# A folded projection product spread over three column groups, last output tiles finished one by one, and a new instruction order

## The chip, the cores and the metric

The kernel runs on one NeuronCore of a Trainium2 chip. Its engines are TensorE (PE in the profile; its weight loads are listed as PEld), VectorE (DVE), ScalarE (ACT), GpSimd (POOL), and SyncE (SP), which here only issues the DMAs. The metric is the device time of one execution in microseconds, lower is better. The median of three runs before the change is 456.12 us (455.83 to 457.48).

## The reference, cut to what matters

Three stages follow each other, on a batch of 2, 768 tokens, 512 channels, all in float32.

```python
# 1. block attention, 8 heads of 64: a window of +-15 keys and 24 block summaries
a = softmax(concat(mask(q @ k.T / 8), q @ k_blockmax.T / 8 + log(32)))
x = a @ concat(v, v_blockmean)
# 2. four causal attention experts, the best two of each token, gated
out = sum_over_chosen_e(w_e * (softmax(causal(x@wq[e] @ (x@wk[e]).T / 8)) @ (x@wv[e]) @ wo[e]))
# 3. mixer: a rank-32 product over the tokens, then an MLP of width 2048
h = (out.T @ U @ V).T          # U is 768 x 32, V is 32 x 768
u = out + h
y = u + relu(u @ w_ch1) @ w_ch2
```

The kernel folds `wo` into what follows it: the rank-32 product is taken on the experts' 256 concatenated head outputs (`C`, 256 x 768 per batch), and `wo @ w_ch1` is computed once. "Folded projection product" below is `U.T @ C.T`, a 32 x 256 result that sums over the 768 tokens.

## The kernel before, in words

Everything is unrolled into some 700 **parts**, small functions of one to twelve **steps** each (a Python generator; a step ends at each `yield`). `at(...)` numbers the parts in the order in which the program names them. The table `TIMES` holds, for each part, the position of each of its steps in one global order, and the instructions are issued in that order. So each engine's instruction stream, and the queue of DMAs on SP, is what the table says; an engine runs its stream strictly in order and waits on semaphores where data isn't ready. `BANKS` names for each part the PSUM bank (of eight, 128 x 512 floats each) that it writes. The constants in `Y` and `Z` give start values for the positions and have no effect where the tables are filled, as they are here.

The parts that matter below, with the line of their TensorE instructions in the profile:

- `vsum` (L333, then L340): block sums of the values of one head pair: 12 products of 128 columns, whose outputs go by turns to the four 32-partition groups of one bank; a copy and a small product add the four groups.
- `a_scores` (L385), `a_trans` (L396), `a_pv` (L408), `a_out` (L424): one 128-query slot of the first attention; 48 slots.
- `qk_proj` (L620), `v_proj` (L569): projections of the experts; after `qk_proj` ACT and DVE split the result in two, and POOL makes four copies (L236).
- `s_row` (L651), `s_norm` (POOL, L675), `t_bank` (L684), `pv` (L704): an expert's attention. `pv` writes by turns to two 64-partition groups of a bank.
- `c_nat` (L722), `a_mat` (L732), `c_add` (L742): the rank-32 product, once per batch. `a_mat` is the folded product: for each of six token tiles a stationary of 128 x 32 (`Usb`) and a moving 128 x 256, accumulated in partitions 0 to 31 of one bank. ACT copies the result twice (L734, L735), DVE takes the rest of it (L739, shown under the helper's line L239), and `c_add` uses all three.
- `w1c` (L497): products that fold `wo` into `w_ch1`; `w1_split`, `w2_split`, `wo_split`, `late_woT`, `v_stack`: splits of loaded weights over DVE, ACT and POOL.
- `resid` (L832), `one` (L810, with ACT L815 and DVE L817), `two` (L823): the MLP. `resid` starts the output bank of a token tile, `one(b, ff, j)` makes 128 hidden channels for 384 tokens, `two(b, ff, j)` adds them to the three token tiles of half `j`. `store` (ACT L843 for even tiles, DVE L845 for odd ones) copies an output bank to SBUF and issues its DMA (L847).

Loads of the first attention, per head pair, by their shapes: keys 416 KB, queries 2 x 192 KB, values 585 KB (for the first pair in two halves of 292.5 KB; the keys there in 144 + 272 KB). Constants: 128 + 180 + 39 KB.

Of the kernel before, what the change touches and what calls it, by code (L numbers as in the profile page):

```python
# [35 lines left out]
def f(ap):  # L36
# [9 lines left out]
         s4=0.55, wc=2.8, cc=1.4, cl=0.4, t3=6.0, t4=5.0, pm0=2.45, pm1=2.09, one=1.3, rl=0.75, rd=0.4, lf=30.0,  # L46
         ls=8.0, lw=-5.0, rs=1.3, rsp=0.4, sto=2.0)
TIMES = [
# [137 lines left out]
N_LAST = 2  # L186
# [4 lines left out]
def tile_block_attention_moe_mixer(ctx: ExitStack, tc: tile.TileContext, qT, kP, vW, vB, wm, woT, wo,  # L191
# [644 lines left out]
    def store(b, t):  # L836
# [5 lines left out]
        if t % 2 == 0:  # L842
            act.copy(sb, ob)  # L843
        else:
            dve.tensor_copy(sb, ob)  # L845
# [240 lines left out]
```

## Time and profile before

| | |
|---|---|
| median of 3 runs | 456.12 us (455.83 to 457.48) |
| the profiled execution's own time | 454.69 us |
| span of its instructions | 452.9 us |
| PE busy | 435.3 us, 96% of the span |
| DVE, ACT, POOL busy | 227.9, 218.3, 179.1 us |
| granted TensorE clock, mean | 0.998 |

The span runs from the first to the last instruction; 1.8 us of the execution's own time lie around it. Busy time is the time in which an engine has an instruction under way. The profile's chain of waits follows the work that ended last back to the start.

### The profile page before, as it was taken

The numbers are of one execution on the slowest core, as the hardware profiler recorded it, in microseconds if no ns is written. First come the engines' busy times: TensorE is split into PE (matmuls) and PEld (weight loads), VectorE is DVE, ScalarE is ACT, GpSimd is POOL, SyncE is SP. The second block draws the span as 40 slices with busy tenths as digits, with TensorE's granted clock in tenths as the row PEclk, the third lists the DMA queues.
The fourth block names the chain that finished last, engine by engine and source line by source line (L and its number), as shares of the span: only waits on it lengthen the run. The fifth ranks groups of instructions, "written<-read, shape, count | busy, mean of one in ns | idle before, by whom it ended". The sixth has DMA issues, their size and how long they took to land.

```text
span 452.9 us, 8633 instructions
## 1 busy us (share of the span) xinstructions
PE 435.3 (96%) x3224; PEld 377.5 (83%) x3224; DVE 227.9 (50%) x629; ACT 218.3 (48%) x578; POOL 179.1 (40%) x252
## 2 busy tenths in 40 slices
PE   1899999999999999899999999999999999999996
PEld 1687898999889887687989889899888888888884
DVE  4578755766557779767884544433322112112112
ACT  3578755756756778787564444434221111111111
POOL 7869853348645799762353143223110000000000
PEclk9999999999999999999999999999999999999999
DMA  8977730000000032253254343302110100000003
GB/s 219 245 214 200 219 88 4 2 1 19 1 2 1 1 111 92 74 187 116 92 168 144 111 150 128 111 31 54 40 69 25 46 2 0 0 1 0 1 0 139
DMA packets 14329, 35.19 MB, mean 78 GB/s; under 512 B 1872, under 2 KB 2896, under 8 KB 14288
## 3 DMA queue, kind: packets, MB, share of 16 engines
q1 hardware_dynamic: 14288, 34.65, 25.4%
q8 instruction: 25, 0.41, 0.4%
q14 instruction: 16, 0.13, 0.1%
HBM read 31.50 MB, written 3.15 MB: 77 GB/s over the span
## 4 chain that ended last, share of the span: by engine, by line
PE 92%; POOL 2%; DMA 2%; DVE 1%; SPq 1%; issue 0%; ACT 0%; DVEq 0%; POOLq 0%; ACTq 0%
PE ps L823 29%; PE ps L810 15%; PE ps L620 7%; PE ps L497 5%; PE ps L385 5%; PE ps L704 4%; PE ps L651 4%; PE ps L569 4%; PE ps L832 4%; PE ps L684 3%; PE ps L408 3%; PE ps L396 3%; PE ps L333 2%; DMA vb<-in_vW_dram 2%; PE ps L424 1%; PE ps L732 1%
## 5 line engine op out<-in xcount | busy, mean ns | idle before, releaser
L817 DVE SCALAR_TENSOR_TENSOR a<-ps,a 128x384 fp32r<-128x384 f32 x64 | 35.1, 555 | 118.4 <-ACT a L815 118.4
L815 ACT ACTIVATE a<-ps 128x384 fp32r<-128x384 f32 x64 | 31.2, 490 | 117.6 <-PE ps L810 62.6
L810 PE MATMUL ps<-x,w1h 128*128 128x384 f32 x256 | 73.5, 337 | 0.1
L823 PE MATMUL ps<-m,a 128*128 128x512 f32 x216 | 52.4, 392 | 0.0
L810 PEld LDWEIGHTS ps<-x,w1h 128*128 128x128 f32 x256 | 47.0, 188 | 2.2 <-DVE a L817 0.4
L823 PEld LDWEIGHTS ps<-m,a 128*128 128x128 f32 x216 | 40.3, 188 | 7.8
L810 PE MATMUL ps<-x,w1l 128*128 128x384 f32 x128 | 43.1, 336 | 0.0
L236 POOL TENSOR_SCALAR a<-a 64x384 fp32r<-64x384 f32 x64 | 33.6, 525 | 23.9 <-ACT a L625 19.5
L620 PE MATMUL ps<-x,m 128*128 128x384 f32 x192 | 36.9, 341 | 0.0
L620 PEld LDWEIGHTS ps<-x,m 128*128 128x128 f32 x192 | 33.1, 188 | 0.5 <-DVE gmx L608 0.2
L651 PE MATMUL ps<-a 128*128 128x384 f32 (+4 forms) x128 | 28.0, 338 | 1.4 <-POOL a L236 1.4
L675 POOL TENSOR_SCALAR ex<-ex,rs,gate 128x256 f32<-128x256 f32 (+5 forms) x36 | 25.9, 726 | 6.0 <-PE ps L704 3.2
L823 PE MATMUL ps<-vb,a 128*128 128x512 f32 x108 | 26.4, 392 | 0.0
L823 PE MATMUL ps<-v,a 128*128 128x512 f32 x108 | 26.4, 395 | 0.0
L257 DVE SCALAR_TENSOR_TENSOR x<-x 128x256 uint32<-128x256 uint32 (+3 forms) x38 | 23.0, 610 | 5.3 <-ACT x L255 5.1
L659 DVE CUSTOM_DVE_ANT_0 ex<-ps,cc 128x512 f32<-128x512 f32 (+5 forms) x36 | 21.1, 597 | 9.1 <-PE ps L651 4.6
L810 PEld LDWEIGHTS ps<-x,w1l 128*128 128x128 f32 x128 | 24.0, 188 | 1.7
L662 ACT ACTIVATE ex<-ex,nmx 128x512 f32<-128x512 f32 (+5 forms) x36 | 23.3, 647 | 3.4 <-DVE nmx L659 3.1
L823 PEld LDWEIGHTS ps<-v,a 128*128 128x128 f32 x108 | 20.2, 188 | 4.2
L388 DVE TENSOR_REDUCE nmx<-ps 128x2 f32<-128x240 f32 x48 | 18.8, 403 | 9.0 <-PE ps L385 7.7
L823 PEld LDWEIGHTS ps<-vb,a 128*128 128x128 f32 x108 | 20.1, 188 | 3.7
L651 PEld LDWEIGHTS ps<-a 128*128 128x128 f32 x128 | 19.9, 189 | 3.5 <-POOL a L236 1.7
(215 smaller groups left out, 924.1 us busy)
## 6 DMA issues: line engine op xcount, KB each, us to landing
x<-in_w_dram SPq DMA_DIRECT2D x16, 512.0 KB, 3.8
x<-in_w_dram SPq DMA_DIRECT2D x20, 256.0 KB, 2.7
vb<-in_vW_dram SPq DMA_DIRECT2D x5, 585.0 KB, 4.7
a<-in_kP_dram SPq DMA_DIRECT2D x7, 416.0 KB, 5.7
out_dram<-a SPq DMA_DIRECT2D x10, 256.0 KB, 2.2
x<-in_wm_dram SPq DMA_DIRECT2D x4, 386.0 KB, 7.0
a<-in_w_dram SPq DMA_DIRECT2D x6, 256.0 KB, 3.1
tb<-in_w_dram SPq DMA_DIRECT2D x6, 256.0 KB, 3.4
```

Source lines behind the costliest of these rows:

```text
L236: pool.tensor_scalar(dst, src, 1.0, 0.0, op0=ALU.mult, op1=ALU.add)
L257: dve.scalar_tensor_tensor(low, high, 3, low, op0=ALU.logical_shift_left, op1=ALU.bitwise_or)
L385: pe.matmul(scb[64 * u:64 * u + 64, hh], QAT[p % NK][hh][:, QT * (2 * t + u):QT * (2 * t + u) + QT], KWT[p % 2][hh][:, 2 * t + u, :], star ...
L497: pe.matmul(acc, wo[k][:, int(a == 2), 128 * c:128 * c + 128], w[k][:, int(a == 1)], start=j == 0, stop=j == 11)
L620: pe.matmul(acc, (WML if wl else WMH)[k][:, 128 * e:128 * e + 128], xt(b, k, xl)[:, c], start=n == 0, stop=n == 11)
L651: pe.matmul(flat[:, base + c0:base + c1], QS[u][:, 128 * i:128 * i + 128], kk[:, c0:c1], start=x == 0, stop=x == 1)
L662: act.activation(ex[:, 0:W], ex[:, 0:W], AF.Exp, bias=nmx, scale=-1.0, accum_out=sums)
L675: pool.tensor_scalar(ex, ex, rs[:, i % 2:i % 2 + 1], gate[b][:, i, e:e + 1], op0=ALU.mult, op1=ALU.mult)
L810: pe.matmul(acc, (W1L if wl else W1H)[ff // 2][:, c, 128 * (ff % 2):128 * (ff % 2) + 128], cp(b, c, xl)[:, o], start=n == 0, stop=n == 5)
L815: act.activation(h, acc, AF.Relu)
L817: dve.scalar_tensor_tensor(l, acc, 0.0, f(h), op0=ALU.max, op1=ALU.subtract)
L823: pe.matmul(out_bank(b, 3 * j + t), a[:, 128 * t:128 * t + 128], w, start=False, stop=ff == 15 and x == 2, skip_group_check=True)
```

## The change

Three edits. (1) `a_mat` sends token tile t to partition group 32 * (t % 3), so three accumulations of two products each take the place of one of six. The three partial results are then added: ACT copies the second to SBUF, DVE adds the first and that copy, then the third; ACT's two copies and DVE's remainder read the SBUF sum instead of PSUM. (2) For batch 1, half 1, the last two `two` parts are cut into one per token tile (`last_two`), and the store of tile 5 is cut into two halves of columns, one copied by ACT and one by DVE. (3) `TIMES` and `BANKS` are replaced as a whole; `t3` changes with them and has no effect of its own.

```diff
-         s4=0.55, wc=2.8, cc=1.4, cl=0.4, t3=6.0, t4=5.0, ...
+         s4=0.55, wc=2.8, cc=1.4, cl=0.4, t3=14.0, t4=5.0, ...
 TIMES = [
...
 BANKS = [
...
     def a_mat(b, bk):
         AST[b] = ast = region("ast", 256)
-        acc = bk[0:32, 0:256]
         for t in range(NT):
-            pe.matmul(acc, Usb[:, t, :], CNAT[b][:, t, :], start=t == 0, stop=t == NT - 1)
-        yield 2 * Y["chl"]
-        act.copy(ast[0:32, :], acc)
-        act.copy(ast[32:64, :], acc)
-        yield Y["chl"]
-        lo_dve(ast[64:96, :], acc, ast[0:32, :])
+            g = 32 * (t % 3)
+            pe.matmul(bk[g:g + 32, 0:256], Usb[:, t, :], CNAT[b][:, t, :], start=t < 3, stop=t >= 3, skip_group_check=True)
+        yield 0.001
+        part, total = (sm.tile([32, 256], F32, name=n, tag=n, bufs=1) for n in ("part", "total"))
+        act.copy(part, bk[32:64, 0:256])
+        yield 0.001
+        dve.tensor_tensor(total, bk[0:32, 0:256], part, op=ALU.add)
+        dve.tensor_tensor(total, bk[64:96, 0:256], total, op=ALU.add)
+        yield 0.001
+        act.copy(ast[0:32, :], total)
+        act.copy(ast[32:64, :], total)
+        yield 0.001
+        lo_dve(ast[64:96, :], total, ast[0:32, :])
...
-    def store(b, t):
+    def store(b, t, on=None, c=slice(0, DM)):
...
+    def last_two(ff, t):
+        mlp2(1, ff, 1, hl[1, ff, 1], (t,))
...
+                if b and j and ff >= 16 - N_LAST:
+                    for t in range(3):
+                        at(T + P * 31 + 0.3 * (N_LAST * t + ff - 16 + N_LAST), last_two, ff, t)
+                else:
+                    at(T + P * u, two, b, ff, j)
...
+            if b and i == NT - 1:
+                at(t, store, b, i, act, slice(0, DM // 2))
+                at(t + 0.01, store, b, i, dve, slice(DM // 2, DM))
+            else:
+                at(t, store, b, i)
```

Read from the two tables, in order of issue, at the places that the prediction speaks of (q0a is the first half of pair 0's queries, and so on):

```
SP at the start, before: cst k0a k0b cst2 q0a vB q0b v0a k1 v0b q1a v1 q1b
                 after:  cst k0a k0b cst2 k1 vB v0a v0b q0a q0b v1 q1a q1b
PE at the start, before: a_scores 0, 1, vsum 0 (L333), a_trans 0, vsum 0 (L340), a_scores 3, 2, 5, a_trans 1, a_scores 4, vsum 1
                 after:  vsum 0 (L333), vsum 0 (L340), a_scores 1, 0, 3, 2, 5, 4, vsum 1, a_trans 0, 1, 3
PE after a_mat 0, before: pv 7 0, pv 7 1, pv 7 2, c_add 0      after: w1c 1 1, pv 7 0, pv 7 2, pv 7 1, c_add 0
PE after a_mat 1, before: resid 0 0, one 0 0 0, c_add 1        after: one 0 0 1, resid 0 0, two 0 0 0, c_add 1
PE at the end, before: two(14, half 1) and two(15, half 1), each tiles 3, 4, 5
               after:  two(14) tile 3, then 14/5, 15/5, 14/4, 15/4, 15/3
copies of the last tiles, before: ACT 4; DVE 5, then 3         after: DVE and ACT 5 in halves, ACT 4, DVE 3
TensorE parts from qk_proj(5, 0) to s_row(7, 5), before: 45    after: 49
```

## Rows read from the trace of the kernel before

**Rows 1.** The page, part 4: shares of the chain that ended last, by engine.

```profile
PE 92%; POOL 2%; DMA 2%; DVE 1%; SPq 1%; issue 0%; ACT 0%; DVEq 0%; POOLq 0%; ACTq 0%
```

**Rows 2.** Windows by stage: stretch, its length, busy us (instructions) per engine, clock, DMA.

```profile
0.00:9.20 9.20, 0.00 (x0) 0.00 (x0) 4.34 (x7) 3.32 (x11) 6.84 (x14) 1.00 0.76 209
9.20:18.70 9.50, 7.84 (x82) 5.76 (x84) 4.47 (x11) 4.00 (x13) 8.56 (x15) 1.00 1.03 251
...
171.00:184.00 13.00, 11.05 (x77) 8.35 (x77) 10.55 (x30) 10.90 (x30) 11.73 (x19) 1.00 0.29 102
...
202.00:215.00 13.00, 13.00 (x81) 8.86 (x81) 8.85 (x21) 10.03 (x24) 2.56 (x2) 1.00 0.32 102
215.00:345.00 130.00, 129.89 (x686) 115.84 (x686) 60.89 (x130) 56.33 (x128) 38.01 (x38) 1.00 0.30 96
345.00:448.40 103.40, 103.36 (x492) 89.61 (x490) 17.61 (x34) 16.25 (x33) 0.00 (x0) 1.00 0.04 16
```

**Rows 3.** The chain of waits, pieces on PE: start us, us, what, instructions.

```profile
18.73 0.80 PE ps L333 x24
...
192.26 1.01 PE ps L704 x7
...
196.32 1.44 PE ps L704 x11
...
202.08 2.71 PE ps L732 x12
...
229.96 1.41 PE ps L832 x6
...
243.90 1.05 PE ps L810 x6
244.95 2.06 PE ps L823 x9
...
248.05 1.39 PE ps L497 x12
```

**Rows 4.** Timeline after the first folded product, ACT and DVE.

```profile
204.82 0.36 ACT L734 CAST ast<-ps 32x256 fp32r<-32x256 f32 x1
...
205.19 0.36 ACT L735 CAST ast<-ps 32x256 fp32r<-32x256 f32 x1
...
205.59 0.42 DVE L239 TENSOR_TENSOR ast<-ps,ast 32x256 fp32r<-32x256 f32 x1 [0.17 <-ACT ast L735]
```

**Rows 5.** Timeline of the end; idle time before an instruction stands in brackets.

```profile
444.01 4.34 PE L823 MATMUL ps<-v,a 128*128 128x512 f32 x18
...
448.39 0.69 DVE L845 COPY x<-ps 128x512 f32<-128x512 f32 x1 [3.10 <-PE ps L823]
449.00 0.68 DVE L845 COPY a<-ps 128x512 f32<-128x512 f32 x1
449.71 0.33 SPq L847 DMA_DIRECT2D out_dram<-a  x1
```

**Rows 6.** Timeline of PE and POOL where PE falls behind.

```profile
147.23 2.28 PE L620 MATMUL ps<-x,m 128*128 128x384 f32 x12
...
150.11 3.64 POOL L236 TENSOR_SCALAR a<-a 64x384 fp32r<-64x384 f32 x6 [0.96 <-ACT a L625]
...
181.88 1.25 POOL L236 TENSOR_SCALAR a<-a 64x384 fp32r<-64x384 f32 x2
...
183.19 0.79 PE L651 MATMUL ps<-a 128*128 128x384 f32 x3 [1.39 <-POOL a L236]
```

**Rows 7.** The chain of waits at the start.

```profile
5.40 6.81 DMA vb<-in_vW_dram
...
12.25 1.51 PE ps L333 x24
...
15.40 2.40 PE ps L385 x24
...
20.44 1.38 PE ps L385 x24
```

More of the change, by code (lines that the diff above doesn't have):

```diff
@@ L45 @@
          ch=55.0, chs=1.8, chl=0.6, te=72.0, vst=0.1, wos=9.0, wot=13.0, f0=97.0, fp=9.0, fk=2.2, wl=-4.0, s2=0.6, s3=0.6,
-         s4=0.55, wc=2.8, cc=1.4, cl=0.4, t3=6.0, t4=5.0, pm0=2.45, pm1=2.09, one=1.3, rl=0.75, rd=0.4, lf=30.0,
+         s4=0.55, wc=2.8, cc=1.4, cl=0.4, t3=14.0, t4=5.0, pm0=2.45, pm1=2.09, one=1.3, rl=0.75, rd=0.4, lf=30.0,
          ls=8.0, lw=-5.0, rs=1.3, rsp=0.4, sto=2.0)
 TIMES = [
[112 rows of a table removed]
[111 rows of a table added]
 ]
 BANKS = [
[21 rows of a table removed]
[22 rows of a table added]
 ]
@@ L817, in mlp1, with mlp2 @@
         dve.scalar_tensor_tensor(l, acc, 0.0, f(h), op0=ALU.max, op1=ALU.subtract)
-    def mlp2(b, ff, j, hl):
+    def mlp2(b, ff, j, hl, tt=range(3)):
         h, l = hl
-        for t in range(3):
+        for t in tt:
             for x, (a, w) in enumerate(((h, W2[ff][0]), (l, W2[ff][0]), (h, W2[ff][1]))):
@@ L841, in store @@
         sb = OB[t % len(OB)]
-        if t % 2 == 0:
-            act.copy(sb, ob)
+        if on is act or on is None and t % 2 == 0:
+            act.copy(sb[:, c], ob[:, c])
         else:
-            dve.tensor_copy(sb, ob)
+            dve.tensor_copy(sb[:, c], ob[:, c])
         yield 0.9
-        nc.sync.dma_start(out[b, 128 * t:128 * t + 128, :], sb)
+        nc.sync.dma_start(out[b, 128 * t:128 * t + 128, c], sb[:, c])
     w2stage = []
@@ L985, in tile_block_attention_moe_mixer @@
                 at(T + P * (u - Y["one"]), one, b, ff, j, u)
-                at(T + P * u, two, b, ff, j)
+                if b and j and ff >= 16 - N_LAST:
[3 more added lines that the diff above has]
+                    at(T + P * u, two, b, ff, j)
             if b == 0:
@@ L993, in tile_block_attention_moe_mixer @@
             out_part[b, i] = at(T + P * j + Y["rsp"] * u - Y["rs"], resid, b, i)
-            at(T + P * (32 if b == 0 else 32 - N_LAST * (1 - j)) + (P * (j - 2) if b == 0 else -P) + Y["sto"] + 0.3 * u, store, b, i)
+            t = T + P * (32 if b == 0 else 32 - N_LAST * (1 - j)) + (P * (j - 2) if b == 0 else -P) + Y["sto"] + 0.3 * u
+            if b and i == NT - 1:
[3 more added lines that the diff above has]
+                at(t, store, b, i)
     for i, (t, u) in enumerate(sorted(accs)):
```

266 rows, old and new, of tables (BANKS, TIMES) are left out of this document.

## Prediction

> **What bounds the kernel now.** I read the chain of waits first. TensorE holds 92% of it [rows 1], so the time is TensorE's work plus the places where it can't go on. The windows by stage say where those are [rows 2]. TensorE has nothing to do for the first 9.2 us. From 171 to 184 us it is busy for 11.05 of 13 us, while POOL is busy for 11.73. From 202 us to 448.4 us it is busy without a gap (13.00 of 13, 129.89 of 130, 103.36 of 103.4). The span goes on to 452.9 us without it. The reader is to see in this that after 202 us work taken off TensorE comes off the end, and work on DVE, ACT and POOL costs nothing so long as it is in time. Both folded products stand there, the first at 202.08 us.
>
> **Three column groups.** One folded product takes 2.71 us for 12 instructions of 256 columns [rows 3]. (Each float32 product is two instructions.) The trace has the same trick elsewhere: a block sum of the values is 24 instructions of 128 columns, as many columns, sent by turns to four partition groups, and it takes 0.80 us, 3.4 times as fast [rows 3]. An expert's `pv` on two groups, 10 instructions of 256 columns and 2 of 128, would take 2.48 us at the folded product's pace and takes 1.44 (the row counts 11 of its 12): 1.7 times [rows 3]. Three groups lie between: 0.80 * 4/3 = 1.07 us by the first, 2.71 / 1.7 = 1.59 us by the second. Both the stationary width of 32 and the turn of the groups are those of the block sum, so I take 1.07 us. That saves 1.64 us a product, 3.3 us for both; bounds 2.2 and 3.8 (the latter if it equalled two full passes, 2.71 / 3). The Trainium skill, "TensorE: Matmul & The Clock Gate", Part 3, gives 2.38 times for three column tiles of 32; the sum would be 3.1 us by it, and no row here shows three.
>
> **The longer way out of it.** Before, two ACT copies of 0.36 us and a DVE step of 0.42 us follow, and the last of them ends 1.22 us after the product (202.08 + 2.71 to 205.59 + 0.42) [rows 3, 4]. The change puts one more ACT copy and two DVE additions of the same 32 x 256 in front, 0.36 + 2 * 0.42 = 1.20 us, so about 2.5 us with hand-offs. TensorE's stream covers this: behind the first product stand a `w1c` (1.39 to 1.43), `pv` 7 0 (some 0.6), `pv` 7 2 (1.44) and `pv` 7 1 (1.01), 4.5 us in all, and behind the second `one` (1.05), `resid` (1.41) and `two` (2.06), again 4.5 us [rows 3]. ACT and DVE run other steps between those of the product (on ACT some 2.1 us after the first), which leaves 0.5 to 1 us of margin. Cost nothing; if the cover fails, `c_add` waits and everything on TensorE behind it, 1 us at most each time. The Trainium skill, "TensorEngine Tiling (Array Packing)", section on performance considerations, speaks against the change here: packing quickens the array and not the emptying of PSUM (rival b). The trace agrees in that the block sums too are followed by a copy and a second product.
>
> **The tail.** TensorE ends at 444.01 + 4.34 = 448.35 us. DVE then copies tile 5 (448.39, 0.69) and only behind it tile 3 (449.00, 0.68), although tile 3's sum was complete two token tiles, some 1.4 us, before the end; the last DMA goes out at 449.71 [rows 5]. In the new order the tiles are completed as 5, 4, 3, and ACT and DVE have copied 5 by the time that 3 is done. One copy is left between the last product and the last DMA: 0.04 + 0.69 + 0.03 = 0.76 us in place of 449.71 - 448.35 = 1.36. That saves 0.6 us. The halving of tile 5 isn't on the path, since tile 3 is last and whole; it costs one more DMA issue of 0.33 us on SP, two tiles ahead of the last. The same 18 products of `two` are merely put in another order.
>
> **The new order: where POOL holds TensorE.** Between `qk_proj`(5, 0) at 147.23 us and `s_row`(7, 5) at 183.19 us TensorE takes 36.0 us, and POOL works without a break worth the name from 150.11 us to the copy that releases `s_row` [rows 6]. Counted along the table with the pieces' times on the chain, the old order has 32.0 us of TensorE parts in this stretch, so about 4 us are lost; POOL's steps there come to 30.7 us by their mean durations. The new order puts the two `qk_proj` of expert step 5 next to each other and 36.9 us of TensorE parts in the stretch against 31.9 us of POOL steps. POOL, at its pace in the trace (36.0 / 30.7), needs 37.4 us, so TensorE would hardly wait. But the part behind it is tighter: up to the first `t_bank` of step 6 the new order leaves TensorE about 1 us less room over POOL than the old one. I take a gain of 1 us, with bounds of a loss of 1 and a gain of 3.5.
>
> **The new order: the start.** The old order starts with two `a_scores` at 9.2 us and then waits for the second half of the values, which land at 12.21; from the end of the block sum and its small product it goes on at 15.40 [rows 7]. The new one loads values before queries, so the block sum comes first. Ahead of the values' second half there are now 1,764 KB instead of 2,147 in SP's queue, so they land at about 12.21 * 1764 / 2147 = 10.0 us; 3.15 us later (12.25 to 15.40) come the scores, at 13.2, if the queries are there: they are now last of the same 2,147 KB, about 12.2 us. Six `a_scores` of 0.80 us each at the start's pace (2.40 for three; 1.38 for three at 20.44, though the windows show a granted clock of 1.00 throughout) end at 18.0 at the latest, then `vsum` 1 starts, against 18.73 before [rows 2, 3, 7]; but two transposes of 0.36 us in all, which stood before it, are now behind it. About 0.3 us are gained. Bounds: 2 us gained if the pace doubles early, 2 lost if the queries come late. I take nothing. Elsewhere in the first attention the two orders keep producers and consumers alike far apart, and I see no reason for either sign; I allow 2 us each way.
>
> **Sum.** 3.3 + 0.6 + 1.0 = 4.9 us. The profiled execution's own 454.69 us become 449.8 (span 452.9 to 448.0); it lies 1.4 us under the median of the runs shown, against which I give the forecast: 456.1 - 4.9 = 451.2 us. Its own range, with the bounds of the single terms taken together (about 2.5 us each way), is 448.7 to 453.7.
>
> **Rivals.**
> (a) The groups don't run side by side, each product stays at 2.71 us and the change does not do what it says: 456.1 - 0.6 - 1.0 = 454.5. Against it stands the block sum's row [rows 3]. Chance 0.04.
> (b) The way out of the product is not covered: `c_add` waits 1 us twice, and the new order gains nothing at POOL: 456.1 - 3.3 - 0.6 + 2 = 454.2. For it: ACT is busy 10.03 of 13 us there; against it: 4.5 us of cover for 2.5 us of work [rows 2, 3, 4]. Chance 0.08.
> (c) The new order gives back 2.5 to 6 us in the first attention or at POOL: 453.7 to 457.2. For it: the whole first attention is re-ordered, where every slot hangs on three engines besides TensorE. Chance 0.10.
> (d) Slower: the first scores stall on the queries, which the new order puts behind the second pair's keys and both halves of the values. They run at 9.2 us now; with the queries at 12.2 us and the half pace until all six are done, the attention starts 3 us later, and if pair 1's values and queries, one place further back too, then hold its slots by another 4 us, 7 us outweigh the 4.9. It decides from 7.2 us of delay at the start on; against it, the old order waits for the values until 12.21 us anyway [rows 7]. 456.1 - 4.9 + 8 = 459.2. Chance 0.06.
> (e) The new order also removes the stall at POOL fully and a part of the waits in the first attention: 2.5 to 5 us more, 446.2 to 448.7. For it: 4 us lost in one stretch alone [rows 6]. Chance 0.17.
>
> **How the numbers follow.** The forecast keeps 0.55. A change of 0.5%, 2.3 us, is about what a measurement of this kernel can tell from none; faster is then under 453.8. The forecast and (e) lie there, and 0.03 of (b), whose waits may be shorter: 0.55 + 0.17 + 0.03 = 0.75. Within 0.5%, up to 458.4, lie (a), (c) and the rest of (b): 0.19. Slower is (d), 0.06. The range of 8 in 10 takes in the forecast's own, half of (e) and most of (a), (b) and (c): 447.3 to 455.0.
>
> **What would show it.** L732's two pieces at about 1.1 us instead of 2.71. DVE's copy of tile 3 directly behind the last product and the last DMA 0.8 us after it. No wait on L742 (`c_add`) over 0.5 us. TensorE busy over 12 of the 13 us before `s_row`(7, 5). TensorE's first instruction L333 at about 10 us, `vsum` 1 between 16 and 18.7. The prediction is wrong if TensorE's idle time before 202 us grows by more than 3 us, or if L732 stays over 1.6.

## The result, and the profile after

The changed kernel took 451.76 us in the median of four runs (450.17 to 453.22), against 456.08 us for the kernel before beside it: a ratio of 0.9898, 95% interval 0.9852 to 0.9945, that is 4.3 us less by the medians and 4.7 us or 1.0% by the ratio. The forecast was 451.2 us. Run again beside the first experiments it took 450.08 us against 456.02, 0.9876 (0.9853 to 0.9899): 5.9 us by the medians, 5.7 by the ratio. The profiled execution after is the slowest of the first four, 453.22 us with a span of 451.4.

Part 4 of the page after, the chain's shares by engine, answers to [rows 1]: POOL's share fell from 2% to 1%.

```profile
PE 94%; DMA 2%; POOL 1%; DVE 1%; SPq 1%; issue 1%; ACT 0%; POOLq 0%
```

The windows after, with the columns of [rows 2] and in its stretches; 184 to 202 us, in which TensorE was busy for 18.00 of 18 us before, is added:

```profile
9.20:18.70 9.50, 4.89 (x52) 3.69 (x54) 5.09 (x10) 2.09 (x8) 7.26 (x11) 1.00 1.04 210
171.00:184.00 13.00, 13.00 (x90) 9.59 (x89) 11.19 (x31) 10.65 (x31) 11.05 (x18) 1.00 0.19 63
184.00:202.00 18.00, 16.38 (x121) 12.93 (x120) 13.85 (x42) 14.18 (x38) 14.56 (x19) 1.00 0.44 147
202.00:215.00 13.00, 13.00 (x102) 10.98 (x100) 10.71 (x23) 10.65 (x25) 2.60 (x3) 1.00 0.24 73
215.00:345.00 130.00, 130.00 (x692) 115.16 (x691) 65.19 (x133) 57.12 (x131) 37.44 (x38) 1.00 0.30 101
```

From 202 us on TensorE is busy without a gap, as before. The 1.95 us of idle time before 184 us in [rows 2], of which 1.39 were a wait for POOL [rows 6], are gone from there, but 1.62 us stand in the next window, 1.37 of them ahead of the piece at 186.67 below. The start looks worse: 4.89 us of work up to 18.7 us instead of 7.84.

TensorE's timeline after (start, length, engine, line, out<-in, number of instructions, in brackets the idle time ahead), the late `s_row` and the first product with what follows it; it answers to [rows 3]:

```profile
186.67 0.85 PE L651 MATMUL ps<-a 128*128 128x320 f32 x4 [1.37 <-DVE nmx L659]
...
203.03 1.06 PE L732 MATMUL ps<-x,Usb 128*32 128x256 f32 x12
204.03 1.34 PE L497 MATMUL ps<-x,v 128*128 128x256 f32 x9
205.21 0.52 PE L497 MATMUL ps<-v,v 128*128 128x256 f32 x3
205.66 3.02 PE L704 MATMUL ps<-pt,vb 128*64 128x256 f32 x24
208.61 0.80 PE L748 MATMUL ps<-vst,ast 96*128 96x384 f32 x3
209.24 1.23 PE L497 MATMUL ps<-x,v 128*128 128x256 f32 x9
```

`c_add` (L748) waits for nothing. The chain of waits has both products (L732), at 0.99 us instead of 2.71:

```profile
203.10 0.99 PE ps L732 x12
...
217.22 0.99 PE ps L732 x12
```

The way out of the first product, on the timelines of ACT and DVE, answers to [rows 4]:

```profile
204.16 0.36 ACT L735 COPY part<-ps 32x256 f32<-32x256 f32 x1 [0.48 <-PE ps L732]
...
205.00 0.42 DVE L738 TENSOR_TENSOR total<-ps,total 32x256 f32<-32x256 f32 x1
...
206.66 0.41 ACT L741 CAST ast<-total 32x256 fp32r<-32x256 f32 x1
...
207.46 0.42 DVE L239 TENSOR_TENSOR ast<-total,ast 32x256 fp32r<-32x256 f32 x1
```

It ends at 207.88, 3.8 us after the product's end at 204.09 and 0.73 us ahead of `c_add` at 208.61; behind the second product 1.1 us are to spare. The end, in the timeline, answers to [rows 5]:

```profile
441.27 6.42 PE L829 MATMUL ps<-v,a 128*128 128x512 f32 x27
447.04 0.59 ACT L849 COPY x<-ps 128x512 f32<-128x512 f32 x1 [0.51 <-PE ps L829]
447.73 0.69 DVE L851 COPY a<-ps 128x512 f32<-128x512 f32 x1 [1.66 <-PE ps L829]
448.45 0.33 SPq L853 DMA_DIRECT2D out_dram<-a  x1
```

The last DMA goes out 0.76 us after the end of the last product (447.69) instead of 1.36. The chain's start answers to [rows 7]:

```profile
4.02 8.65 DMA vb<-in_vW_dram
...
12.80 1.54 PE ps L333 x24
...
20.90 0.80 PE ps L333 x24
```

The values' second half took 8.65 us to land and came at 12.67, and `vsum` 1 started 2.2 us later than before (18.73). Whether that is the order's doing one pair of profiles can't say; the experiments' profiles below can.

### The profile page after: what moved, and what is told of

The parts are those of the page before. It is cut to its first block, busy times and chain, and to the rows that moved or that the text cites. A ratio compares the mean times of both kernels' runs of the same rounds, so it can differ in the third digit from the quotient of the medians.

```text
span 451.4 us, 8626 instructions
## 1 busy us (share of the span) xinstructions
PE 432.3 (96%) x3224; PEld 376.2 (83%) x3224; DVE 233.7 (52%) x633; ACT 219.1 (49%) x581; POOL 178.4 (40%) x252
## 4 chain that ended last, share of the span: by engine, by line
PE 94%; DMA 2%; POOL 1%; DVE 1%; SPq 1%; issue 1%; ACT 0%; POOLq 0%
PE ps L829 29%; PE ps L816 15%; PE ps L620 8%; PE ps L385 5%; PE ps L704 5%; PE ps L497 5%; PE ps L651 4%; PE ps L684 4%; PE ps L569 4%; PE ps L838 4%; PE ps L408 3%; PE ps L396 3%; DMA vb<-in_vW_dram 2%; PE ps L333 2%; PE ps L424 1%; PE ps L340 1%
## 5 line engine op out<-in xcount | busy, mean ns | idle before, releaser
L823 DVE SCALAR_TENSOR_TENSOR a<-ps,a 128x384 fp32r<-128x384 f32 x64 | 35.0, 556 | 114.6 <-ACT a L821 114.6
L675 POOL TENSOR_SCALAR ex<-ex,rs,gate 128x256 f32<-128x256 f32 (+5 forms) x36 | 25.9, 729 | 10.9 <-DVE rs L670 7.5
L257 DVE SCALAR_TENSOR_TENSOR x<-x 128x256 uint32<-128x256 uint32 (+3 forms) x38 | 24.7, 653 | 2.5 <-ACT x L255 2.4
L662 ACT ACTIVATE ex<-ex,nmx 128x256 f32<-128x256 f32 (+5 forms) x36 | 23.4, 652 | 4.8 <-DVE nmx L659 4.4
L659 DVE CUSTOM_DVE_ANT_0 ex<-ps,cc 128x256 f32<-128x256 f32 (+5 forms) x36 | 21.1, 598 | 6.3 <-PE ps L651 4.1
L651 PEld LDWEIGHTS ps<-a 128*128 128x128 f32 x128 | 19.9, 189 | 3.7 <-DVE nmx L659 2.2
```

What stands on the lines that cost most here:

```text
L257: dve.scalar_tensor_tensor(low, high, 3, low, op0=ALU.logical_shift_left, op1=ALU.bitwise_or)
L651: pe.matmul(flat[:, base + c0:base + c1], QS[u][:, 128 * i:128 * i + 128], kk[:, c0:c1], start=x == 0, stop=x == 1)
L662: act.activation(ex[:, 0:W], ex[:, 0:W], AF.Exp, bias=nmx, scale=-1.0, accum_out=sums)
L675: pool.tensor_scalar(ex, ex, rs[:, i % 2:i % 2 + 1], gate[b][:, i, e:e + 1], op0=ALU.mult, op1=ALU.mult)
L823: dve.scalar_tensor_tensor(l, acc, 0.0, f(h), op0=ALU.max, op1=ALU.subtract)
```

## The experiments

The tables of order were edited by a few lines behind them (`TIMES[u] = ...` for part number u).

**The changed kernel once more**, unedited. 

> The changed kernel once more, for a second profile and more executions: its four executions fall into two pairs, near 450.4 and 453.1 us, and the profile at hand is of the upper pair. Theory (start): the pairs differ by when TensorE gets going, since after 204 us nothing on TensorE waits; a profile near a span of 448.6 us would show the first block sum or the sixth first score 2 to 3 us earlier than the 12.80 us and 20.90 us of the profile at hand. Rival (clock or POOL): the start is the same and the 2 to 3 us lie between 84 and 204 us. Median of the executions 450 to 453 us.

450.08 us (449.11 to 452.5). In its profile, span 449.1, the values landed 7.09 us after their issue and `vsum` 1 started 1.6 us earlier than in the profile above: the same program, and 1.6 of the 2.3 us between the two spans. So the theory has the larger part; 1.3 us more lie between `vsum` 1 and the first product, where the rival looked for it, and 0.5 us are lost again behind that (table below).

**The product in one group again, all else as changed.** DVE takes a maximum of equal operands where it added partial sums, so that the way out keeps its length.

```diff
-            g = 32 * (t % 3)
-            pe.matmul(bk[g:g + 32, 0:256], Usb[:, t, :], CNAT[b][:, t, :], start=t < 3, stop=t >= 3, skip_group_check=True)
+            pe.matmul(bk[0:32, 0:256], Usb[:, t, :], CNAT[b][:, t, :], start=t == 0, stop=t == NT - 1)
```

> The changed kernel with the six products of the folded projection one after the other in one partition group, as before the change; the copy and the two DVE steps stay (a maximum with itself in place of the sum), and so does the order. Theory: the groups save what the trace shows, 2 x 1.72 us, all of it on the chain: 3.4 us slower than the changed kernel, about 455.2. Rival (the order pays, the grouping is covered by something else): within 1 us of the changed kernel.

454.33 us, 0.996 (0.9941 to 0.9979) of before, 3.8 us more than the changed kernel by the ratios. In the new order the grouping is worth what it takes off TensorE (3.4 us), and the new order and tail without it are worth some 1.7 us.

**The grouped product alone, in the old order**: the new `a_mat`, its three ACT and DVE steps at the place of the first old copy.

```diff
+for _u, _t in [(409, (1256, 1270, 1270.3, 1270.6, 1274)), (417, (1305, 1317, 1317.3, 1317.6, 1321))]:
+    TIMES[_u] = _t
```

> The kernel before with the grouped product alone: old order, old banks, old tail; the new steps of the product are placed between its old ones. Theory: the same 3.4 us off the end, about 452.7 us. Rival (the longer way out isn't covered in the old order, where 3 to 3.5 us of TensorE work stand between product and use): a wait on c_add of up to 1 us each time, 453.7 to 454.7. Rival (the new order is what pays): 455.5 to 456.5.

456.02 us, 0.9997 (0.9982 to 1.0013): nothing gained, though the product takes 1.06 us here too. Its timelines of PE and ACT, from the slowest of its twelve executions (458.2 us):

```profile
204.24 1.06 PE L734 MATMUL ps<-x,Usb 128*32 128x256 f32 x12
...
207.09 0.36 ACT L737 COPY part<-ps 32x256 f32<-32x256 f32 x1
...
209.39 0.41 PE L750 MATMUL ps<-vst,ast 96*128 96x384 f32 x1 [0.83 <-DVE ast L241]
210.20 0.65 PE L724 MATMUL ps<-cc,x 128*128 128x128 f32 x4 [0.40 <-DVE x L710]
...
213.11 2.25 PE L499 MATMUL ps<-x,v 128*128 128x256 f32 x9
...
219.87 0.77 PE L750 MATMUL ps<-vst,ast 96*128 96x384 f32 x3 [0.52 <-ACT w1h L503]
```

and its windows:

```profile
209.00:212.00 3.00, 1.95 (x11) 1.49 (x12) 2.38 (x6) 2.90 (x7) 1.70 (x2) 0.97 0.00 0
212.00:216.00 4.00, 4.00 (x24) 3.65 (x26) 2.38 (x6) 2.26 (x6) 0.86 (x1) 0.60 0.79 260
```

The first copy out (L737) runs 1.8 us after the product, behind ACT's other steps. `c_add` waits 0.83 us, `c_nat` (L724) behind it, and after these pauses the granted clock has a mean of 0.60 over four microseconds: TensorE ran at 1.2 GHz, the lower of its two levels, for most of them. A `w1c` piece that takes 1.23 us in the changed kernel takes 2.25.

The fall of the clock costs some 1.6 us in this execution (4 us x 0.40), but it isn't what ate the gain. Seven of the twelve executions had a mean granted clock of 0.998 or more, and their median is 455.42 us; that of the five others (0.994 to 0.996) is 457.35. Without the fall the grouping alone still gains only 0.6 of the 3.4 us; in the profile at hand TensorE is idle for 2.1 of the 28 us from 203 to 231, mostly at the waits above.

**The same, with the way out issued directly behind the product**, to part the place in ACT's queue from the cover on TensorE.

```diff
-for _u, _t in [(409, (1256, 1270, 1270.3, 1270.6, 1274)), (417, (1305, 1317, 1317.3, 1317.6, 1321))]:
+for _u, _t in [(409, (1256, 1256.1, 1256.2, 1256.3, 1256.4)), (417, (1305, 1305.1, 1305.2, 1305.3, 1305.4))]:
```

> The kernel before, with the grouped product, TensorE's order untouched, and the five steps of the product's way out (one ACT copy, two DVE additions, two ACT copies, one DVE remainder) issued directly behind the product instead of at their old place. Theory 1, place in ACT's queue: with the old place the first ACT copy ran 1.8 us after the product's end, behind ACT steps of the splits of w1 and w2. Issued directly, it runs 0.4 to 0.7 us after it and c_add finds its operands: 456.0 - 3.3 = about 452.7. Theory 2, cover on TensorE: what counts is that 3.3 us of pv stand behind the product and the way out takes longer whatever its place; then the waits at c_add stay and the time is 455.5 to 456. A median of 454.3 or less speaks for theory 1, 455 or more for theory 2.

461.75 us, 1.0121 (1.0083 to 1.0158), slower than either theory had it. Its timelines:

```profile
204.78 0.36 ACT L737 COPY part<-ps 32x256 f32<-32x256 f32 x1 [1.36 <-PE ps L734]
205.18 0.41 DVE L739 TENSOR_TENSOR total<-ps,part 32x256 f32<-32x256 f32 x1 [3.25 <-ACT part L737]
...
208.78 3.86 PE L706 MATMUL ps<-pt,vb 128*64 128x256 f32 x20 [3.26 <-ACT pt L694]
...
220.22 0.73 PE L840 MATMUL ps<-woh,x 128*128 128x512 f32 x2 [2.28 <-DVE x L241]
```

The copy does run at once, but ACT idles for 1.36 and DVE for 3.25 us ahead of it, waiting in order, and the `pt` copies behind it on ACT reach `pv` 3.26 us late. With each of the two long waits on TensorE the granted clock falls (window, length, busy us of PE, PEld, DVE, ACT, POOL, then the mean clock):

```profile
208.00:212.00 4.00, 3.22 (x18) 2.06 (x19) 2.98 (x7) 3.44 (x8) 1.42 (x2) 0.57 0.00 0
...
222.00:226.00 4.00, 4.00 (x16) 4.00 (x15) 3.02 (x8) 0.85 (x2) 0.00 (x0) 0.57 0.00 0
```

That costs up to 2 x 4 us x 0.43 = 3.4 us. In the window from 203 to 231 us TensorE is idle for 5.9 us. Both together, less the 3.4 us of the grouping, make 5.9; measured are 5.5 by the ratio. The mean granted clock was 0.993 to 0.996 in all six executions, so the fall belongs to each of them. Theory 1 falls for this place: what is passed on the way is needed as well. Places between the two weren't run.

**The same, with the old place of the way out and more TensorE work ahead of `c_add`** (part 451 is w1c(1,1), 418 to 420 are three parts of c_add 1, 441 is w1c(0,1), whose bank w1c(1,1) takes).

```diff
+for _u, _t in [..., (418, (1338.5, 1341.1, 1352, 1366)), (419, (1340.5, 1359, 1364, 1369)), (420, (1338.6, 1341.2, 1342.2, 1353)), (441, (1199, 1259, 1259.5)), (451, (1270.5, 1313, 1318))]:
+    TIMES[_u] = _t
+for _u, _b in [(451, 2)]:
+    BANKS[_u] = _b
```

> The kernel before, with the grouped product, the way out at its old place in the queues of ACT and DVE, but more TensorE work between product and c_add: a w1c (1.9 us) behind the first, and one(0,0,1), one(0,1,0) and resid(0,1) (3.5 us) behind the second. Theory 2, cover on TensorE: both waits on c_add go and the gain of the grouping, 3.3 us, comes out: about 452.7. Theory 1, place in ACT's queue: the 0.83 us wait of the first c_add goes too, since 1.9 us more stand in front, but what is queued behind it (the transposes of the second product's input waited 0.4 and 0.26 us on DVE) stays: 453.5 to 454.5. If neither wait is what ate the gain, it stays at 456.

456.56 us, 1.0028 (1.0001 to 1.0056): no gain. The wait of the first `c_add` is gone, as both theories had it, and the granted clock stays at 1.00, but other waits stand behind it, and TensorE is busy for 25.18 of the 28 us from 202 to 230:

```profile
213.01 1.06 PE L736 MATMUL ps<-x,Usb 128*32 128x256 f32 x12 [0.80 <-ACT x L730]
...
216.58 0.44 PE L820 MATMUL ps<-x,w1h 128*128 128x384 f32 x1 [0.91 <-DVE w1l L243]
...
223.13 0.44 PE L752 MATMUL ps<-vst,ast 96*128 96x384 f32 x1 [0.76 <-DVE x L755]
```

The second product waits for the transposes' copies, `one` for a split weight, `c_add` for DVE. So it isn't the wait at the first `c_add` alone that holds the old order: ACT and DVE are late at several places. From the first product to the second TensorE had 9.31 us of work before (202.00 to 211.31); that the two engines can't keep up with 1.7 us less of it is my reading. In the changed kernel 14.12 us lie between the two products (203.03 to 217.15), since two `one`, two `resid` and a `w1c` were put there. No run changed this distance by itself.

**The changed kernel without its cover**: w1c(1,1) ahead of the first product, two(0,0,0) ahead of the second. In it resid(0,0) starts the bank of token tile 0 after two(0,0,0) has added to it, so that this tile lacks the share of the first 128 hidden channels; the same instructions run.

```diff
+for _u, _t in [(451, (1254.5, 1332, 1337)), (513, (1322.5,))]:
+    TIMES[_u] = _t
```

> The changed kernel, with the cover taken away and nothing else: w1c(1,1), 1.86 us, goes from behind the first product to ahead of it, and two(0,0,0), 2.06 us, from behind the second product to ahead of it. Cover theory: the way out of the product ends 3.8 us after the first product and c_add stands 4.5 us behind it, 0.73 us to spare; without the w1c c_add waits 1.1 us; at the second the room is 1.1 us and two(0,0,0) is worth 2.06, so 1.0 us is lost there: 2.1 us slower than the changed kernel, 452.2 to 453. Rival: ACT and DVE then have less queued between the steps of the way out, and it ends as much sooner: less than 0.7 us slower.

453.2 us, 0.9938 (0.9923 to 0.9953), 2.8 us slower than the changed kernel by the ratios of the two jobs (0.9876). TensorE's timeline:

```profile
206.41 0.77 PE L750 MATMUL ps<-vst,ast 96*128 96x384 f32 x3 [0.20 <-DVE ast L241]
...
222.17 0.77 PE L750 MATMUL ps<-vst,ast 96*128 96x384 f32 x3 [0.96 <-ACT a L823]
```

The second wait is as expected (1.0); ACT's step of `one` (L823) ended it at 222.15, and the way out itself had ended 0.13 us earlier. The first is 0.2 instead of 1.1: there the way out did end sooner. By the table below, with the 1.63 us of the moved `w1c` (204.03 to 205.66 after) added, 245.72 + 1.63 - 244.66 = 2.7 us are lost behind the first product; the idle time in the windows from 202 to 230 us makes 1.4 of it, the rest I can't place.

**The old order up to the first `c_nat` (173 us), the new one behind it.** The edit gives 373 parts the places, and 239 the banks, that this takes.

```diff
+for _u, _t in [(0, (-9914,)), (1, (-9987,)), (2, (-9810,)), ...]:
+    TIMES[_u] = _t
+for _u, _b in [(20, 0), (21, 0), (22, 0), ...]:
+    BANKS[_u] = _b
```

> The changed kernel, with the order and the banks of the kernel before for everything issued ahead of the first c_nat (173 us), so the first attention and the experts up to step 6 run as before, and the new order, the grouped product and the new tail act only behind it. Theory: the gain lies in the order around the two products, which covers their way out: 456.0 - 3.4 - 0.6 = 452.0, half a us to either side. Rival: the order of the first 170 us carries part of it, or the two orders don't fit where they meet and POOL makes TensorE wait there: 453.5 or more.

453.51 us, 0.9949 (0.9931 to 0.9967). Behind the first product it is as fast as the changed kernel (244.23 us to the last product's end, table below). But where the two orders meet TensorE waits, longest here:

```profile
178.41 0.45 PE L688 MATMUL ps<-cc,vb 128*128 128x128 f32 x1 [2.01 <-DVE nmx L663]
```

The profile is that of the slowest of the twelve executions (456.1 us), and behind this wait its granted clock has a mean of 0.57 over four microseconds, which costs it up to 1.7 us:

```profile
178.00:182.00 4.00, 3.59 (x16) 1.84 (x17) 3.22 (x10) 1.54 (x4) 2.72 (x5) 0.57 0.17 60
```

By its time the rival holds (453.5 or more). By stage the theory holds behind the product and the rival ahead of it; how long TensorE waits where the orders meet in a median execution no profile shows.

**The start of the kernel before, all else as changed**: order, loads and banks up to `vsum` 1.

```diff
+for _u, _t in [(1, (-9987,)), (3, (-9998, -9997, -9995)), (4, (-9993, -9989, -9983)), ...]:
+    TIMES[_u] = _t
```

> The changed kernel with the old order (and banks) of everything before the second block sum, its loads included; behind that the new order. Theory: the new start costs about 2.2 us (the second block sum at 20.90 us in the new profile, 18.73 in the old), so this is 1.5 to 2.5 us faster than the changed kernel, about 449.5 us. Rival (the attention stage catches up because it is held by its loads or by other engines): within 0.7 us of the changed kernel, and the first product of the experts at the same time as there.

450.87 us, 0.989 (0.9871 to 0.9908), not faster than the changed kernel: the rival holds. My reading of the first two profiles, that the new start costs 2 us, falls.

**Values ahead of the second pair's keys.**

```diff
+for _u, _t in [(192, (27.5, 42))]:
+    TIMES[_u] = _t
```

> The changed kernel, with the load of the second pair's keys (416 KB) issued behind the values and the first half of the queries instead of ahead of the values. Theory of the prediction, loads land in the order of issue after the bytes ahead of them: the values' second half lands 416 KB at some 219 GB/s, 1.9 us, earlier, and TensorE's first instruction L333, seen at 11.2 to 12.8 us in the changed kernel, comes at 9.3 to 10.9; the time falls by up to 1.9 us. Rival, loads in flight share the bandwidth: the keys still take their share, so L333 moves by 0.5 us (one issue earlier) to 1 us and the time by less than 0.8 us.

453.21 us, 0.9936 (0.9918 to 0.9954), slower, which neither theory had. The timelines of PE and DVE:

```profile
9.28 1.51 PE L335 MATMUL ps<-vb,cc 96*32 96x128 f32 x24 [9.28 <-DMA vb<-in_vW_dram]
...
11.96 0.95 DVE L356 TENSOR_REDUCE ks<-a 128x24 f32<-128x768 f32 x1 [3.52 <-DMA a<-in_kP_dram]
...
15.20 0.62 PE L342 MATMUL ps<-vt,cc 128*24 128x128 f32 x2 [4.41 <-DVE vt L339]
```

On the loads the prediction's theory holds: with 416 KB less ahead the block sum starts at 9.28, at the early end of the 9.3 to 10.9 expected. But DVE's stream has the block maximum of the late keys (L356) ahead of the block sum's copy (L339), and TensorE waits 4.41 us for that.

**The same, with that maximum moved behind the block sum** (part 190, ksum 1):

```diff
+for _u, _t in [(192, (27.5, 42)), (190, (48.5, 54.1, 54.2, 67, 74, 80, 83))]:
+    TIMES[_u] = _t
```

> The changed kernel, with the second pair's keys loaded behind the values and the first half of the queries, as in the run before, and now also with their block maximum (ksum 1 on DVE, and its first two POOL steps) behind the first pair's block sum, so that no engine's stream waits for these keys ahead of the first scores. Theory, loads land after the bytes ahead of them, and what went wrong was DVE's stream: L333 starts at 9.3 us, as it did in the run before, goes on without the 4.41 us wait, the second block sum starts at 17 to 18 us in place of 19.3 to 20.9, and the time is 448.0 to 449.5, 1 to 2 us under the changed kernel. Rival, another load or stream sets the start (the queries' second half, or POOL, which now has the 1.3 us of ksum 1 later and delays the vb and key copies behind it): the second block sum stays at 19 us or later and the time at 450 to 452.

450.35 us, 0.9884 (0.9865 to 0.9904): not to be told from the changed kernel. TensorE's timeline:

```profile
8.99 1.51 PE L335 MATMUL ps<-vb,cc 96*32 96x128 f32 x24 [8.99 <-DMA vb<-in_vW_dram]
...
14.08 0.67 PE L387 MATMUL ps<-c,ex 128*64 128x120 f32 x4 [1.45 <-issue]
```

The block sum came at 8.99, but the second scores' operand `c` was written by a DVE copy that ended at 13.97, again behind the maximum (11.89 to 12.84), and `vsum` 1 started at 18.67, 0.6 us earlier than in the better profile of the changed kernel. By its time the rival holds; 18.67 lies between what the two had. The six scores between took 0.80 us each, the slow pace of the start [rows 7], though the block sum had come 2.2 us earlier than there.

**Other work between the two `s_row` that share banks** (pv(4,0) and s_row(7,1), against the wait of 1.37 us at 186.67).

```diff
+for _u, _t in [(332, (1142.7, 1164)), (388, (1142.8, 1182, 1186))]:
+    TIMES[_u] = _t
```

> The changed kernel, with pv(4,0) and s_row(7,1), 1.0 us of TensorE work, put between s_row(7,5) and s_row(7,4), which write the same two banks one behind the other; in the changed kernel TensorE waited 1.1 to 1.4 us there for DVE's read of the first. Theory: that wait goes, 1.0 to 1.4 us less than the changed kernel, 448.8 to 449.2 if that is at 450.1. Rival: POOL, which releases the t_bank of expert step 6 behind it, holds TensorE anyway, so the wait only moves there: same time as the changed kernel, within 0.3 us.

450.47 us, 0.988 (0.9847 to 0.9912), no change: the rival holds. The wait on DVE is gone, and the next `t_bank` waits for POOL instead:

```profile
186.52 0.98 PE L686 MATMUL ps<-cc,ex 128*128 128x128 f32 x7 [0.71 <-POOL ex L677]
```

**The kernel before with its last two DVE copies exchanged**:

```diff
+for _u, _t in [(691, (1876, 1879)), (695, (1877, 1880))]:
+    TIMES[_u] = _t
```

> The kernel before, with only the two last DVE copies and their stores exchanged: tile 3 first, tile 5 last. The tail theory: a copy of 0.7 us goes from behind the last product to ahead of it, the last DMA goes out 0.75 us after the last product instead of 1.36: 456.0 - 0.6 = 455.4 without any cutting of the last products or of the store. Rival: the two halves of the token tiles are complete at the same time, so nothing is gained: 456.0.

455.78 us, 0.9996 (0.9976 to 1.0017): 0.6 us can't be told from none here. In the timeline SP now issues three stores at the end, one behind the other, the last 0.91 us after the last product (449.39):

```profile
449.40 0.33 SPq L849 DMA_DIRECT2D out_dram<-x  x1
...
449.82 0.38 SPq L849 DMA_DIRECT2D out_dram<-a  x1
450.30 0.41 SPq L849 DMA_DIRECT2D out_dram<-x  x1
```

The last issue comes 0.45 us earlier, but the span ends only 0.07 us nearer to the last product (4.45 us after it instead of 4.52, table below): this store lands 2.51 us after its issue instead of 2.14, with two others just ahead of it. So one copy less behind the last product brings almost nothing by itself. In the changed kernel the two halves of tile 5 are issued before the last product ends, and about 580 KB are left to move after it (157 GB/s over 3.7 us) instead of 790 (175 GB/s over 4.5 us).

**All profiles by stage.** Worked out from the timelines: the start of `vsum` 1; from there to the first product's start; on to the end of the last product; from there to the trace's last instruction.

```
kernel                                vsum 1   to product 1   to last product   rest
before                                18.66    183.34         246.35            4.52
  copies exchanged                    19.66    183.38         246.35            4.45
  product grouped                     21.05    183.19         247.65            4.54
  grouped, way out early              20.14    183.52         252.52            4.54
  grouped, more cover                 20.33    183.26         247.37            4.53
changed, first profile                20.83    182.20         244.66            3.75
changed, second profile               19.25    180.91         245.18            3.75
  product in one group                20.77    181.31         248.08            3.74
  old start                           19.86    180.57         244.65            3.76
  values first                        21.70    181.47         244.65            3.75
  values first, maximum later         18.67    181.30         244.66            3.75
  work between the s_row              19.44    180.80         244.65            3.74
  without cover                       19.20    182.72         245.72            3.75
  old order up to 173 us              20.64    185.70         244.23            3.75
```

One `w1c`, 1.43 us to the start of the next part (209.24 to 210.67), stands ahead of the first product in the old order and behind it in the new; to compare them it goes off the second column of before and onto the third (181.91 and 247.78). Three of the profiles hold a fall of the clock: grouped (third column), grouped with the way out early (third) and the old order up to 173 us (second).

## Why the prediction was right

**Three column groups: right.** Forecast 1.07 us a product and 3.3 us for both; measured 0.99 and, between the changed kernel and the same with one group, 248.08 - 244.66 = 3.42 us. The Trainium skill's 2.38 times ("TensorE: Matmul & The Clock Gate", Part 3) is under the 2.71 / 0.99 = 2.7 of this trace; by it the sum had been 3.1. My upper bound of 3.8 doesn't follow from its bracket: 2.71 / 3 a product gives 3.6.

**The longer way out: cost nothing, as forecast, but by less than I thought and with a wrong price for failure.** I had it at 2.5 us against 4.5 us of cover; it takes 3.8, since ACT and DVE run other steps between its own, and 0.73 us are to spare. And where the cover fails the loss isn't "1 us at most each time": in the old order nothing of the 3.4 us is left in the median, and 0.6 in the executions without a fall of the clock; in the new order without cover 2.8 us are lost. The waits don't stay at `c_add`, and the granted clock can fall after them (0.60 over four microseconds). Rival (b) is thus what the grouping alone does. The Trainium skill, "TensorEngine Tiling (Array Packing)", performance considerations, says that packing doesn't quicken the emptying of PSUM. The traces agree: a copy of 32 x 256 out of it takes 0.36 us before and after, and in the old order nothing was gained (0.9997). I set the chance of (b) by counting the cover in the new order, and that was the right count for this change.

**The tail: right in size, by a step that isn't all of it.** 0.6 us forecast, from 1.36 to 0.76 measured at the last issue; from the last product to the last instruction it is 0.8 less (4.52 to 3.75). I had put all of it down to the copy behind the last product. With one of the two copies there moved ahead in the old order the last issue came 0.45 us earlier and the end 0.07, so that the stores still under way count as well. The new tail by itself wasn't run.

**POOL and the new order: right in sign, mis-sized.** Forecast 1.0 us. To the first product the new order needs 181.29 us in the mean of six profiles (180.57 to 182.20; the edits that touch this stretch left out) against 181.91: 0.6 us. Behind the product, with one group in both, it needs 0.3 us more than the old one (248.08 against 247.78). My sign that TensorE would be busy for over 12 of the 13 us ahead of `s_row`(7, 5) was met, 13.00, and yet little was gained: the idle time moved behind it (186.67), and when the wait on DVE there is taken away, 0.71 us stay, at POOL.

**The start: right in its sum, by a wrong step.** I had the values landing at 10.0 us by the bytes up to and with them (both totals, 1,764 and 2,147 KB, count the half itself). In five profiles with the new order of loads the block sum started at 10.79 to 12.80, 11.7 in the mean; in seven with the old order at 12.25 to 14.03, 12.9 in the mean. So the order of loads gives 1.2 us and not the 2.2 that the bytes made, and it doesn't reach `vsum` 1, which starts at 19.9 in the mean of the five and 20.0 of the seven: from the block sum to there the new order takes 7.9 to 8.4 us (8.0 forecast) and the old one 6.4 to 7.4, since two of the six scores stood ahead of the block sum in it. Taking nothing was right, also as the second block sum starts outside my 16 to 18.7. What I compared with, 12.25 and 18.73 in the profile of before, was the earliest of seven.

**The sum.** 3.4 for the groups, 0.8 for the tail, 0.6 - 0.3 for the order, 0.1 for the start: 4.6 us by these profiles against 4.9 forecast; measured 4.7 by the ratio and, in the second comparison, 5.7. That the sum lies so near is in part luck: the order gave 0.3 us instead of 1.0 and the tail 0.2 more than forecast. Of the rivals, (a) and (d) are refuted by the product's 0.99 us and by the old start's 450.87 us. (c) and (e) are not seen. What stays open: which part of the new order gives the 0.6 us, what the tail gives alone, and 1.6 us that the old order with more cover loses beyond its idle time on record (2.8 us), as the new one without cover loses 1.3 beyond its 1.4.

## What to carry to other kernels

When a faster instruction makes its result's way out longer, count the work of the other engines between the two points on TensorE, not the one wait: two products 1.7 us shorter each gained nothing in the old order, all of their 3.4 us in the new one, and 2.8 us less than that when two pieces of work behind them were moved ahead. A load or an in-order step that is moved can hold up everything behind it; list each engine's stream past the new place first. Don't take the end of a kernel to be its last issue: stores under way count too. Compare a start that waits for loads over several profiles: with one program the second block sum varied by 1.6 us. Look at the granted clock of every execution, not of the profiled one alone, before a loss is put down to waits.

## What the runs showed of the hardware that I had not expected

The same load, issued at 4.0 us as the last of the same 1,764 KB, took 6.66, 7.09, 7.37, 8.23 and 8.65 us to land in five executions; as the last of 1,348 KB, issued at 3.54, it took 5.32 and 5.61. Three accumulations of 32 columns in column groups of the array ran 2.7 times as fast as one behind the other. In three profiles the granted clock fell from 2.4 to 1.2 GHz in mid-kernel: after pauses of up to 0.83 us with TensorE busy for 1.95 of 3 us (a mean of 0.60 over four microseconds), and at or behind single waits of 3.26, 2.28 and 2.01 us (0.57 each). With waits of 0.28 to 0.91 us in the run with more cover, and with one of 1.37 us in the changed kernel, it stayed at 1.00. At the start TensorE's pieces took longer than the same pieces later (three scores 2.40 us against 1.38 in [rows 7], a block sum 1.51 against 0.80), where the windows print a clock of 1.00: there the lengths of the pieces tell the pace and the printed clock doesn't.
